# Row sums laid along the output by TensorE instead of by way of DRAM, in a fused attention and two-MoE kernel

## The chip, the cores and the metric

The kernel runs on one core of a Trainium2 chip. Its time is the device time of one execution in microseconds (us), the median of several runs. The core has five instruction streams that run side by side and meet by semaphores: TensorE (PE in the profile, its weight loads PEld), VectorE (DVE), ScalarE (ACT), GpSimd (POOL), and SyncE (SP), which here only issues DMAs. Each stream is issued in its own order.

## The reference

Three layers follow each other. Attention keeps, in each row of scores, those that are not below the 32nd largest, and takes the softmax over them:

```python
scores = scale * np.matmul(q, k.transpose(0, 1, 3, 2))        # 4 batches, 8 heads, 576 x 576, head_dim 64
kth = np.partition(scores, -32, axis=-1)[..., -32:-31]
scores = np.where(scores >= kth, scores, -1000000000.0)
attn = np.exp(scores - np.max(scores, axis=-1, keepdims=True))
attn = attn / (np.sum(attn, axis=-1, keepdims=True) + 1e-09)
x = np.matmul(attn, v)                                        # becomes 2304 tokens x 512
x = (x @ w_a) * (x @ w_b) @ w_out                             # first MoE layer, d_ff 1536
# second layer: each token goes to the best of 8 experts by a normalised dot product:
out[mask] = gate_w[mask, None] * (np.maximum(x[mask] @ w1[e], 0.0) @ w2[e])
```

The change lies in the division by the row sum and in what stands around it.

## The kernel before, in words

Work is laid out in three stretches of one program: attention with the first MoE layer in its gaps, the rest of the first MoE layer with routing, and the experts.

Attention goes by pairs of heads and by *parts* of a batch. A part (`prep`, line 268) is one pair of heads and 256 query columns ("A", "B"), with 64 more where it has a tail ("T"); the order of parts stands in `SEQ` (line 28), four pairs for each entry, 32 parts in all, 16 of them with a tail. A part without a tail has 4 *row blocks* of 128 queries, one with a tail has 5; there are 144 row blocks. One *step* of the main loop (line 820) takes one row block through each of its stages, each stage at another distance:

- `scores` (348), two steps ahead: two halves of 288 columns, matmuls into PSUM and an eviction by ScalarE (364). The halves use the pool `sc` of one bank, all other PSUM tiles of attention (turns of K and Q, turns of weights, mix) share the pool `tr` of `NTR = 3` banks. Two further pools of two banks belong to the MoE layer.
- `topk` (367), at the step itself and the next: four MAX8 and three MATCH_REPLACE8 over 576 columns on DVE, then the threshold (389). Row n's first half and row n-1's second half are issued alternately (lines 849 to 852).
- `softmax` (391), two steps later: Relu on ScalarE (396) makes a penalty, POOL negates the maximum (397) and subtracts the penalty (398), ScalarE takes the exponential and sums it into `o.sm` (400).
- `turn` (402), three steps later up to step 18, then four (`TL0`, `TL`, `S1`): five transposes by PE in two tiles (417), evicted into `o.wt` (420).
- `mix` (438), in the step after the last turn of the part: 10 matmuls with V, evicted to `o.xsb` (449). The first four parts (`F0 * NP`) run it at once.
- `sums` (423), three steps after the last row of a part, at the head of DVE's work of that step: add 1e-9 (428), reciprocal (429). The result lies with queries on partitions, the output of `mix` has queries along columns. So the reciprocals are stored to DRAM, transposed (430), and read back by one or two DMAs that repeat them over 64 partitions each (433, 436) into `o.xR`.
- `finish` (455), `LATE = 2` steps after `mix`: POOL multiplies `xsb` by `xR` (457), splits the product into two float32r parts, and SyncE stores them (466, 467) for the first MoE layer. Four pairs of a batch's part finished make a group of tokens ready.

Within a step the order is written out by hand (lines 841 to 925, under `manual_schedule`): loads of V (841), `sums` and `topk` (845 to 852), K and Q work, then five slots (892): first tile of turns, first half of scores, second tile of turns, mix, second half of scores. `soft` is the generator of `softmax`: its first part (Relu, negation, subtraction) is issued after slot 0, the exponential after slot 2. After every piece, `background` (752) issues matmuls of the first MoE layer from a budget per step (`STEP`). SyncE issues in the order of the program too, except where a priority moves a DMA ahead.

Other names that the trace shows: raw weights of the first MoE layer arrive by L496 and are converted by DVE (516, 518), ScalarE (519) and POOL (523, 533) until 330 us; the split weights go to `wab_d` in DRAM and come back as `wab` for each group of 256 tokens (589); `xg` (577) are a group's tokens; L650 are the matmuls with `wab`; `route` (673) stores rows at L707.

Of the kernel before, what the change touches and what calls it, by code (L numbers as in the profile page):

```python
# [10 lines left out]
F32 = mybir.dt.float32  # L11
# [17 lines left out]
LAG = 2  # L29
AHEAD_L = 8  # L30
TL = 4
LATE = 2
STEP = 4.8
TL0 = 3
S1 = 19
F0 = 1
# [46 lines left out]
def fused_kernel(  # L83
# [37 lines left out]
    xl_d = drm.tile([P, NP, NT], F32, name="xl_d")  # L121
    wab_d = drm.tile([2, NF, P, 2 * KC * P], F32, name="wab_d")
    kT_d = drm.tile([B * NP, P, 2 * S], F32, name="kT_d")
    rc_d = drm.tile([3 * B * NP, 5, P], F32, name="rc_d")
    row_d = drm.tile([NT + 1, RW], F32, name="row_d")
    ids_d = drm.tile([NE * STRIDE, 2], I32, name="ids_d")

# [69 lines left out]
    with ExitStack() as ph:  # L197
        wk = ph.enter_context(tc.tile_pool(name="wk", bufs=2, side="right"))
        ps = ph.enter_context(tc.tile_pool(name="ps", bufs=2, space=PSUM, side="right"))
        NTR = 3  # L200

        fill = wk.tile([P, S], F32, name="z", bufs=ZB).bitcast(I32)[:, : NE * STRIDE * 2 // P]
        dve.memset(fill, NT)
# [144 lines left out]
        def scores(t):  # L348
            o = t.o
            t.s = wk.tile([P, S], F32, name="s", bufs=SB)  # L350
            for j in range(2):
                if j and t.n == 0:
                    p = ps.tile([P, 512], F32, name="tr", bufs=NTR)[:, :288]
                else:
                    p = ps.tile([P, 288], F32, name="sc", bufs=1)
                cs = slice(j * 288, (j + 1) * 288)
                if t.kind == 2:
                    terms = [(o.qm[:, a, h, :], o.kT[:, h, cs]) for h in range(2) for a in range(2)]
                else:
                    off = (2 * t.kind + t.c) * P  # L360
                    terms = [(o.qT[:, a, off : off + P], o.kT[:, t.kind, cs]) for a in range(2)]
                for i, (l, r) in enumerate(terms):
                    pe.matmul(p, l, r, start=(i == 0), stop=(i == len(terms) - 1))  # L363
                act.activation(t.s[:, cs], p, AF.Copy, scale=SCALE)  # L364
                yield 0.12 * len(terms)
# [55 lines left out]
                yield 0.107 * n5  # L421

        def sums(o):

            o.xR = wk.tile([P, 320], F32, name="xR", bufs=2)
            d = rc_d[o.n]
            sl = slice(0 if o.M else 4, 5 if o.tail else 4)
            dve.tensor_scalar(o.rc[:, sl], o.sm[:, sl], 1e-9, None, op0=OP.add)
            dve.reciprocal(o.rc[:, sl], o.rc[:, sl])
            sp.dma_start(d[sl].rearrange("c p -> p c"), o.rc[:, sl])  # L430
            if o.M:
                src = d[0:4].rearrange("(h c) p -> h (c p)", h=2)
                sp.dma_start(o.xR[:, :256], src.unsqueeze(1).to_broadcast([2, 64, 256]))
            if o.tail:
                src = d[4].rearrange("(h j) -> h j", h=2)
                sp.dma_start(o.xR[:, o.M : o.N], src.unsqueeze(1).to_broadcast([2, 64, 64]))

        def mix(o):
            N = o.N
            o.xsb = wk.tile([P, 320], F32, name="xsb")  # L440
            o.xh = wk.tile([P, 320], F32R, name="xh", bufs=1)
            p = ps.tile([P, 512], F32, name="tr", bufs=NTR)
            for c in range(5):
                ks = slice(0, P) if c < 4 else slice(64, P)
                for h in range(2):
                    pe.matmul(  # L446
                        p[h * 64 : h * 64 + 64, :N], o.vs[ks, h, c], o.wt[h][ks, c, :N], start=(c == 0), stop=(c == 4)
                    )
            act.activation(o.xsb[:, :N], p[:, :N], AF.Copy)
            later(now[0] + LATE, finish, o)  # L450
            yield N / 100

# [352 lines left out]
        def later(step, fn, *args):  # L805
            due.append((step, fn, args))
# [10 lines left out]
        cur = none  # L817
        thresholds = [none]
        coming = []
        for step in range(-AHEAD_L, NRW + TL + 5):  # L820
            now[0] = step
            if step + AHEAD_L < NRW:
# [7 lines left out]
            if 0 <= step + AHEAD_P < NRW:  # L830
# [7 lines left out]
                o.left += 1  # L838
                live[step + AHEAD_P] = Rows(o, kind, c, slot)
                live[step + AHEAD_P].n = step + AHEAD_P  # L840
            for ahead, todo_v in ((1, load_v),):
                if 0 <= step + ahead < NRW and rows[step + ahead][3]:
                    with tc.high_priority(offset=FG):
                        todo_v(made[rows[step + ahead][:3]])
            with tc.high_priority(offset=FG):
                if 0 <= step - 3 < NRW and rows[step - 3][4]:
                    sums(live[step - 3].o)
                if 0 <= step < NRW:
                    cur = topk(live[step], FOLD[step % len(FOLD)])
                for _ in range(4):  # L850
                    next(thresholds[0], None)
                    next(cur, None)
                if step == NRW:
                    thresholds[0] = none
                elif 0 <= step < NRW:
                    thresholds[0] = cur
# [13 lines left out]
                    coming.pop(0)  # L870
            while 0 <= step + AHEAD_Q < NRW and live[step + AHEAD_Q].o in flips:
                flip_next()
            soft = softmax(live[step - 2]) if 0 <= step - 2 < NRW else none
            i = step - (TL0 if step < S1 else TL)
            if i != turned[0] + 1:
                i = -1
# [15 lines left out]
            for slot_, g in enumerate((tg, sg, tg, mg, sg)):  # L892
# [1 line left out]
                    mixes.pop(0)  # L894
                    mg = none
                with tc.high_priority(offset=FG):
                    if slot_ in (0, 2):
                        next(soft, None)
                    if slot_ < 3:
                        conv.stage()  # L900
# [348 lines left out]
```

## Time and profile before

| | us |
|---|---|
| median of 3 runs | 1520.99 (1520.69 to 1521.65) |
| the profiled execution's own time | 1534.14 |
| its span, first to last instruction | 1532.3 |
| PE busy | 1211.9 (79%) |
| DVE busy | 927.3 (61%) |
| ACT busy | 790.1 (52%) |
| POOL busy | 755.2 (49%) |

The page also shows the span in 40 slices of 38.3 us; each digit is the busy share of a slice in tenths, for PEclk the granted clock, for DMA the mean share of the 16 DMA engines:

```profile
PE   4566666658688787878778797877999997999997
DVE  6979668758688777978686888911100013554451
ACT  4655555556565666666555575633433233444441
POOL 5655567765454655655565556544444432112210
PEclk9856777779899989999899899978999999999999
DMA  6432356566468856575587875927987823645440
```

DVE's high digits end in slice 26, near 1000 us: there the last row block is over. Attention takes the first 1045 us with its last stores; PE's nines after that are the rest of the first MoE layer and the experts. An engine's busy share is an average over such stages, and idle time of an engine that nobody waits for costs nothing.

### The profile page before, as it was taken

What the parts mean: (1) busy time and instruction counts of PE and PEld (TensorE: products, weight loads), DVE (VectorE), ACT (ScalarE), POOL (GpSimd) and SP (SyncE); (2) the same over time, 40 slices, a digit from 0 to 9 for tenths busy, and PEclk for the clock granted to TensorE, in tenths of its full rate; (3) what the DMA queues carried; (4) which work ended last, traced back from release to release, by engine and by line L of the source; (5) the groups of instructions that cost most, each with busy time, mean ns of one, the idle gap of its engine ahead of it and who ended that gap; (6) DMA issues with size and microseconds to landing.
All of it is one profiled execution on the core that took longest, in us unless ns stands there. A gap on an engine that the chain in (4) does not pass through costs nothing. (4 is left out here: it accounts for less than half of the span.)

```text
span 1532.3 us, 22337 instructions
## 1 busy us (share of the span) xinstructions
PE 1211.9 (79%) x7400; PEld 1010.9 (66%) x7401; DVE 927.3 (61%) x2022; ACT 790.1 (52%) x1885; POOL 755.2 (49%) x1164
## 2 busy tenths in 40 slices
PE   4566666658688787878778797877999997999997
PEld 3444554546566666767656576756888886888886
DVE  6979668758688777978686888911100013554451
ACT  4655555556565666666555575633433233444441
POOL 5655567765454655655565556544444432112210
PEclk9856777779899989999899899978999999999999
DMA  6432356566468856575587875927987823645440
GB/s 200 122 86 60 123 141 155 176 185 146 128 182 131 131 148 167 156 211 131 123 152 148 181 144 149 181 68 259 318 288 232 244 73 112 204 165 177 158 139 17
DMA packets 150889, 241.75 MB, mean 158 GB/s; under 512 B 43853, under 2 KB 96205, under 8 KB 150770
## 3 DMA queue, kind: packets, MB, share of 16 engines
q1 hardware_dynamic: 146610, 230.00, 56.2%
q0 software_dynamic: 4160, 10.29, 2.1%
q8 instruction: 59, 0.97, 0.4%
q14 instruction: 60, 0.49, 0.2%
HBM read 200.10 MB, written 40.93 MB: 157 GB/s over the span
## 5 line engine op out<-in xcount | busy, mean ns | idle before, releaser
L650 PE MATMUL ab<-xg,wab 128*128 128x256 f32 x2592 | 406.9, 303 | 77.0 <-DMA wab<-wab_d 45.1
L650 PEld LDWEIGHTS ab<-xg,wab 128*128 128x128 f32 x2592 | 362.2, 204 | 93.6 <-DMA wab<-wab_d 28.5
L398 POOL TENSOR_TENSOR z<-s,z 128x576 f32<-128x576 f32 x144 | 205.7, 1428 | 260.3 <-ACT z L396 252.9
L384 DVE MAX8 t<-y 128x8 f32<-128x576 f32 x432 | 311.3, 748 | 3.1
L363 PE MATMUL sc<-kT,qT 128*128 128x288 f32 x510 | 148.6, 374 | 107.8 <-ACT s L364 100.9
L387 DVE MATCH_REPLACE8 y<-t,y 128x576 f32<-128x576 f32 x288 | 213.9, 743 | 0.0
L363 PEld LDWEIGHTS sc<-kT,qT 128*128 128x128 f32 x510 | 94.7, 223 | 151.4 <-ACT s L364 132.3
L417 PE MATMUL tr<-ident,z 128*128 128x128 f32 x720 | 150.1, 313 | 54.9 <-ACT z L400 29.9
L400 ACT ACTIVATE z<-z,bi 128x576 f32<-128x576 f32 x144 | 111.2, 772 | 123.9 <-POOL z L398 122.9
L420 ACT ACTIVATE wt<-tr 128x384 f32<-128x384 f32 (+2 forms) x320 | 127.8, 413 | 42.1 <-PE tr L417 39.3
L417 PEld LDWEIGHTS tr<-ident,z 128*128 128x128 f32 x720 | 99.7, 159 | 69.9 <-ACT z L400 33.0
L621 PE MATMUL x<-wo,gh 128*128 128x512 f32 x432 | 141.4, 410 | 0.0
L364 ACT ACTIVATE s<-sc 128x288 f32<-128x288 f32 x287 | 116.1, 405 | 25.8 <-PE sc L363 24.3
L1032 PE MATMUL y<-u,hT 128*128 128x512 f32 (+1 forms) x528 | 128.0, 396 | 0.4 <-DVE hT L1137 0.4
L384 DVE MAX8 t<-s 128x8 f32<-128x576 f32 x144 | 107.1, 744 | 30.9 <-ACT s L364 30.9
L955 DVE TENSOR_TENSOR u<-raw,u 128x1024 fp32r<-128x1024 f32 x64 | 76.3, 1221 | 79.1 <-ACT u L954 79.0
L1004 POOL DMA_INDIRECT out_dram<-o,ids x24 | 24.1, 1005 | 199.0 <-ACT o L1003 197.1
L659 POOL TENSOR_TENSOR gab<-gab 128x256 f32<-128x256 f32 x108 | 81.7, 756 | 80.3 <-ACT gab L654 64.3
L446 PE MATMUL tr<-wt,vs 128*64 128x256 f32 (+3 forms) x640 | 113.9, 502 | 1.8 <-ACT kT L321 1.1
L396 ACT ACTIVATE z<-s,bi 128x576 f32<-128x576 f32 x144 | 112.3, 780 | 0.3 <-DVE bi L389 0.3
L1032 PEld LDWEIGHTS y<-u,hT 128*128 128x128 f32 (+1 forms) x528 | 89.8, 174 | 27.5 <-DVE hT L1137 0.5
L387 DVE MATCH_REPLACE8 y<-t,s 128x576 f32<-128x576 f32 x144 | 106.9, 743 | 0.0
(169 smaller groups left out, 1912.5 us busy)
## 6 DMA issues: line engine op xcount, KB each, us to landing
wab<-wab_d SPq DMA_DIRECT2D x192, 512.0 KB
raw<-in_moe_w_dram SPq DMA_DIRECT2D x28, 1024.0 KB
wab_d<-wab SPq DMA_DIRECT2D x24, 512.0 KB
kT_d<-kT SPq DMA_DIRECT2D x16, 576.0 KB
kT<-kT_d SPq DMA_DIRECT2D x16, 576.0 KB
vs<-in_v_dram SPq DMA_DIRECT2D x32, 256.0 KB
raw<-in_moe_w_a_dram SPq DMA_DIRECT2D x12, 512.0 KB
raw<-in_moe_w_b_dram SPq DMA_DIRECT2D x12, 512.0 KB
```

What stands on the lines that cost most here:

```text
L363: pe.matmul(p, l, r, start=(i == 0), stop=(i == len(terms) - 1))
L364: act.activation(t.s[:, cs], p, AF.Copy, scale=SCALE)
L384: dve.max(v, cur)
L387: dve.match_replace(out=rest, in_to_replace=v, in_values=cur, imm_value=LOWEST)
L396: act.activation(t.w, t.s, AF.Relu, bias=t.bi[:, 1:2], scale=-HUGE)
L398: pool.tensor_tensor(t.w, t.s, t.w, op=OP.subtract)
L417: pe.transpose(pt[:, i * P : (i + 1) * P], t.w[:, k0 : k0 + P], ident)
L420: act.activation(th[:, sl, w], pv[:, :, src], AF.Copy)
L446: pe.matmul(p[h * 64 : h * 64 + 64, :N], o.vs[ks, h, c], o.wt[h][ks, c, :N], start=(c == 0), stop=(c == 4))
L621: pe.matmul(px[t], g[:, ts], wo[:, w, f], start=(f == 0 and i == 0), stop=(f == NF - 1 and i == 2))
L650: pe.matmul(p[:, i], wt[:, a, c, :], xg[x][:, c, :], start=(j == 0), stop=(j == len(terms) - 1))
L1032: pe.matmul(p[:m], (hi, lo)[a], u[:, b, f % 4, :], start=(f == 0 and i == 0), stop=(f == NF2 - 1 and i == 2))
```

## The change

Reciprocals no longer go through DRAM: `rc_d` and its 32 stores and 48 reads are gone. A new function `along`, called in `mix` after the eviction, makes matmuls whose stationary operand is a column of reciprocals repeated 64 times and whose moving operand is the identity, so that each of 64 output partitions gets the reciprocals along its columns; ScalarE copies the result into `o.xR`. `sums` keeps its two DVE instructions and is called five steps after a part's last row, three for the first four parts. The exponential of a row is issued at the head of the next step, before `sums` and `topk`, and the first part of `softmax` after slot 1. V's load is issued two steps after a part's first row, and one step ahead of it as before only for the first two parts. `finish` follows in the step of `mix` (`LATE = 0`). Scores take their tiles from `tr`, which has four banks now; `sc` is gone.

```diff
@@ -29,7 +29,7 @@
 LAG = 2
 AHEAD_L = 8
 TL = 4
-LATE = 2
+LATE = 0
 STEP = 4.8
 TL0 = 3
 S1 = 19
@@ -121,7 +121,6 @@
     xl_d = drm.tile([P, NP, NT], F32, name="xl_d")
     wab_d = drm.tile([2, NF, P, 2 * KC * P], F32, name="wab_d")
     kT_d = drm.tile([B * NP, P, 2 * S], F32, name="kT_d")
-    rc_d = drm.tile([3 * B * NP, 5, P], F32, name="rc_d")
     row_d = drm.tile([NT + 1, RW], F32, name="row_d")
     ids_d = drm.tile([NE * STRIDE, 2], I32, name="ids_d")
 
@@ -197,7 +196,7 @@
     with ExitStack() as ph:
         wk = ph.enter_context(tc.tile_pool(name="wk", bufs=2, side="right"))
         ps = ph.enter_context(tc.tile_pool(name="ps", bufs=2, space=PSUM, side="right"))
-        NTR = 3
+        NTR = 4
 
         fill = wk.tile([P, S], F32, name="z", bufs=ZB).bitcast(I32)[:, : NE * STRIDE * 2 // P]
         dve.memset(fill, NT)
@@ -349,10 +348,7 @@
             o = t.o
             t.s = wk.tile([P, S], F32, name="s", bufs=SB)
             for j in range(2):
-                if j and t.n == 0:
-                    p = ps.tile([P, 512], F32, name="tr", bufs=NTR)[:, :288]
-                else:
-                    p = ps.tile([P, 288], F32, name="sc", bufs=1)
+                p = ps.tile([P, 512], F32, name="tr", bufs=NTR)[:, :288]
                 cs = slice(j * 288, (j + 1) * 288)
                 if t.kind == 2:
                     terms = [(o.qm[:, a, h, :], o.kT[:, h, cs]) for h in range(2) for a in range(2)]
@@ -421,19 +417,27 @@
                 yield 0.107 * n5
 
         def sums(o):
-
-            o.xR = wk.tile([P, 320], F32, name="xR", bufs=2)
-            d = rc_d[o.n]
             sl = slice(0 if o.M else 4, 5 if o.tail else 4)
             dve.tensor_scalar(o.rc[:, sl], o.sm[:, sl], 1e-9, None, op0=OP.add)
             dve.reciprocal(o.rc[:, sl], o.rc[:, sl])
-            sp.dma_start(d[sl].rearrange("c p -> p c"), o.rc[:, sl])
-            if o.M:
-                src = d[0:4].rearrange("(h c) p -> h (c p)", h=2)
-                sp.dma_start(o.xR[:, :256], src.unsqueeze(1).to_broadcast([2, 64, 256]))
-            if o.tail:
-                src = d[4].rearrange("(h j) -> h j", h=2)
-                sp.dma_start(o.xR[:, o.M : o.N], src.unsqueeze(1).to_broadcast([2, 64, 64]))
+
+        def along(o):
+
+
+            p = ps.tile([P, 512], F32, name="tr", bufs=NTR)
+            for s in range(0 if o.M else 2, 3 if o.tail else 2):
+                for h in range(2):
+                    w, src, js = (s * P, 2 * h + s, slice(0, P)) if s < 2 else (o.M, 4, slice(h * 64, h * 64 + 64))
+                    n = js.stop - js.start
+                    pe.matmul(
+                        p[h * 64 : h * 64 + 64, w : w + n],
+                        o.rc[js, src : src + 1].to_broadcast([n, 64]),
+                        ident[js, js],
+                        start=True,
+                        stop=True,
+                    )
+            o.xR = wk.tile([P, 320], F32, name="xR", bufs=2)
+            act.activation(o.xR[:, : o.N], p[:, : o.N], AF.Copy)
 
         def mix(o):
             N = o.N
@@ -447,6 +451,7 @@
                         p[h * 64 : h * 64 + 64, :N], o.vs[ks, h, c], o.wt[h][ks, c, :N], start=(c == 0), stop=(c == 4)
                     )
             act.activation(o.xsb[:, :N], p[:, :N], AF.Copy)
+            along(o)
             later(now[0] + LATE, finish, o)
             yield N / 100
 
@@ -817,6 +822,7 @@
         cur = none
         thresholds = [none]
         coming = []
+        soft = none
         for step in range(-AHEAD_L, NRW + TL + 5):
             now[0] = step
             if step + AHEAD_L < NRW:
@@ -838,13 +844,18 @@
                 o.left += 1
                 live[step + AHEAD_P] = Rows(o, kind, c, slot)
                 live[step + AHEAD_P].n = step + AHEAD_P
-            for ahead, todo_v in ((1, load_v),):
-                if 0 <= step + ahead < NRW and rows[step + ahead][3]:
+            for ahead in (1, -2):
+                j = step + ahead
+                if 0 <= j < NRW and rows[j][3] and (made[rows[j][:3]].n < 2) == (ahead == 1):
                     with tc.high_priority(offset=FG):
-                        todo_v(made[rows[step + ahead][:3]])
+                        load_v(made[rows[j][:3]])
             with tc.high_priority(offset=FG):
-                if 0 <= step - 3 < NRW and rows[step - 3][4]:
-                    sums(live[step - 3].o)
+                next(soft, None)
+                soft = softmax(live[step - 2]) if 0 <= step - 2 < NRW else none
+                for back in (3, 5):
+                    j = step - back
+                    if 0 <= j < NRW and rows[j][4] and (made[rows[j][:3]].n < F0 * NP) == (back == 3):
+                        sums(made[rows[j][:3]])
                 if 0 <= step < NRW:
                     cur = topk(live[step], FOLD[step % len(FOLD)])
                 for _ in range(4):
@@ -870,7 +881,6 @@
                     coming.pop(0)
             while 0 <= step + AHEAD_Q < NRW and live[step + AHEAD_Q].o in flips:
                 flip_next()
-            soft = softmax(live[step - 2]) if 0 <= step - 2 < NRW else none
             i = step - (TL0 if step < S1 else TL)
             if i != turned[0] + 1:
                 i = -1
@@ -894,7 +904,7 @@
                     mixes.pop(0)
                     mg = none
                 with tc.high_priority(offset=FG):
-                    if slot_ in (0, 2):
+                    if slot_ == 1:
                         next(soft, None)
                     if slot_ < 3:
                         conv.stage()
```

## Rows read from the trace of the kernel before

**Rows 1.** Windows view: window, us, busy PE, PEld, DVE, ACT, POOL (instructions); clock, DMA share, GB/s.
```profile
150.00:400.00 250.00, 156.26 (x873) 128.56 (x875) 179.38 (x373) 137.64 (x320) 162.19 (x189) 0.75 0.56 153
400.00:1000.00 600.00, 490.09 (x3248) 400.15 (x3246) 488.80 (x1123) 375.56 (x979) 346.03 (x573) 0.92 0.68 153
```

**Rows 2.** SyncE's waits, 0 to 1045: who for whom, us in total, times, longest.
```profile
SPq L433 <- DMA rc_d<-rc: 250.5, 26, 11.4
SPq L430 <- DVE rc L429: 64.4, 24, 7.6
...
SPq L259 <- PE tr L446: 51.9, 12, 10.9
```

**Rows 3.** Timeline of SyncE, 202 to 217: start, us, issue.
```profile
204.68 0.38 SPq L430 DMA_DIRECT2D rc_d<-rc  x1
...
206.44 0.37 SPq L496 DMA_DIRECT2D raw<-in_moe_w_out_dram  x1
...
214.82 0.51 SPq L433 DMA_DIRECT2D xR<-rc_d  x1
```

**Rows 4.** Timeline of DVE, 203 to 222; in brackets the idle time before and its end.
```profile
219.35 0.43 DVE L516 TENSOR_SCALAR w64t<-raw 128x512 int32<-128x512 int32 x1 [9.77 <-DMA raw<-in_moe_w_out_dram]
```

**Rows 5.** Waits of all engines, 400 to 1000 (columns as in rows 2).
```profile
DVE rc L428 <- ACT z L400: 84.5, 17, 13.9
...
ACT z L400 <- POOL z L398: 72.4, 61, 6.5
```

**Rows 6.** The page's costliest groups: count, busy us, mean ns, idle before, releaser.
```profile
L396 ACT ACTIVATE z<-s,bi 128x576 f32<-128x576 f32 x144 | 112.3, 780 | 0.3 <-DVE bi L389 0.3
```

**Rows 7.** PE's waits, 400 to 1000.
```profile
PE sc L363 <- ACT s L364: 59.8, 69, 4.5
PE ab L650 <- DMA wab<-wab_d: 25.8, 8, 7.7
```

**Rows 8.** DVE's waits, 150 to 400.
```profile
DVE w64t L516 <- DMA raw<-in_moe_w_out_dram: 27.7, 3, 9.8
...
DVE w64t L516 <- DMA raw<-in_moe_w_a_dram: 14.0, 5, 9.4
```

**Rows 9.** PE's waits, 150 to 400.
```profile
PE ab L650 <- DMA wab<-wab_d: 10.8, 1, 10.8
```

**Rows 10.** Timeline of SyncE, 988 to 1045.
```profile
999.26 0.52 SPq L433 DMA_DIRECT2D xR<-rc_d  x1
...
1000.40 0.37 SPq L707 DMA_DIRECT2D row_d<-xr  x1
```

**Rows 11.** Waits of all engines, 1000 to 1045.
```profile
POOL xr L706 <- DMA row_d<-xr: 11.4, 1, 11.4
...
POOL xsb L457 <- DMA xR<-rc_d: 10.4, 1, 10.4
```

**Rows 12.** Groups by shape, 0 to 1045, and L449's copies (min/median/max ns).
```profile
L417 PE MATMUL tr<-ident,z 128*128 128x128 f32 x720 | 150.1, 313 | 54.9 <-ACT z L400 29.9 <-ACT wt L420 20.9 <-ACT xsb L449 2.5
...
L446 PEld LDWEIGHTS tr<-wt,vs 128*64 128x64 f32 x512 | 42.7, 173 | 39.8 <-issue 20.3 <-PE sc L363 2.3 <-ACT kT L321 1.9
...
L449 ACT ACTIVATE xsb<-tr x32: 361/401/439, 61.7 to 1030.3; 128x256 f32<-128x256 f32 x16, 128x320 f32<-128x320 f32 x16
```

**Rows 13.** Waits of all engines, 0 to 150.
```profile
PE tr L417 <- ACT z L400: 26.7, 12, 3.6
...
DVE rc L428 <- ACT z L400: 11.2, 4, 4.3
```

**Rows 14.** Windows view of the hundred us in which DVE is busiest after 150.
```profile
900.00:1000.00 100.00, 84.49 (x565) 68.74 (x566) 91.22 (x215) 65.28 (x164) 56.47 (x105) 0.93 0.77 162
```

**Rows 15.** Timelines of DVE (ends of row blocks) and PE (a mix), 608 to 626.
```profile
614.89 0.13 DVE L389 TENSOR_SCALAR bi<-t 128x1 f32<-128x1 f32 x1
...
619.98 0.13 DVE L389 TENSOR_SCALAR bi<-t 128x1 f32<-128x1 f32 x1
...
623.33 2.53 PE L446 MATMUL tr<-wt,vs 128*64 128x256 f32 x20
```

## The prediction, made before the result was known

> **What bounds the kernel now.** I read the stage table first, then SyncE's own waits, then the compute engines' waits stage by stage.
>
> In attention's second stage, 150 to 400 us [rows 1], no engine is above 72% (DVE 179.38, POOL 162.19 of 250) and PE's granted clock is 0.75, between its levels of 1.2 and 2.4 GHz: everybody waits. From 400 to 1000 PE is busy 490.09 and DVE 488.80 of 600, at 0.92: two engines at 82% that hold each other up.
>
> Who holds them up stands in SyncE's waits [rows 2]: 250.5 us before L433, for the store of the row sums (L430) to land before they are read back, 26 waits of 9.6 us; 64.4 before L430 itself, for DVE's reciprocal; 51.9 before V's load (L259), for the mix that still reads the old buffer. SyncE issues in order, so for a third of the 1045 us every other load is queued behind these three. In one case [rows 3] the store goes out at 204.68, the read-back at 214.82, and a load of raw weights, issued at 206.44 right behind the store, lets DVE go on only at 219.35 [rows 4], 12.9 us later, after 9.77 us of idle time. So the store delays also what is already issued.
>
> DVE's own biggest wait is another one: 84.5 us in 17 times from 400 to 1000 before the sums' addition (L428), for the part's last exponential [rows 5]. It looks like the prize, and I do not count it as one: the sums stand at the head of DVE's step, and ScalarE's Relu, which consumes what DVE makes, waited for DVE 0.3 us in all 144 rows [rows 6]. DVE is early; it stalls there because ScalarE and PE are late, and if only the sums moved it would stall a little later.
>
> What makes those two late from 400 to 1000: 72.4 us of ScalarE before the exponential [rows 5], for POOL's subtraction issued half a step earlier; 59.8 us of PE before scores, for the eviction of the single `sc` bank, and 25.8 for the first MoE's weights [rows 7].
>
> **The change part by part.** The sum is made against the profiled run's own time, 1534.14 us (span 1532.3); the median of 1520.99 is 0.9914 of it, and I scale at the end.
>
> 1. *The DRAM exchange goes* (32 stores, 48 reads), and V's load moves, for all but the first two parts, behind the mix that frees its buffer; so the waits at L433, L430 and most of L259 leave SyncE. V's two DMAs go three steps back in its order, past K's, Q's and the weights' loads; the mix wants them six or seven steps later, some 30 us, so this costs nothing. What is late next is the load itself; a loss I exclude, since the same bytes move in fewer DMAs.
> 150 to 400: DVE's waits for raw weights are 27.7 + 14.0 = 41.7 us [rows 8], PE's for weights 10.8 [rows 9]. Bounds: 52.5 if all go; 10.8 if only PE's counts, because POOL's conversions would take the time anyway. I take 35, nearer the upper: DVE, PE and ScalarE stand together, but a load that no exchange delays still takes time.
> 400 to 1000: 25.8 us of PE [rows 7]; bounds 0 and 25.8; I take 22.
> 1000 to 1045: the row store at L707 goes out at 1000.40, directly behind the read-back of 999.26 [rows 10], and POOL waits 11.4 us for it; then the last read-back keeps POOL 10.4 us [rows 11]. No row work is left to cover these. Bounds 10 and 21.8; I take 18.
>
>    Against this stands a rule. The Trainium skill, DMA: Bandwidth & Descriptors, section "Latency and other measured facts", puts the fixed cost of a DMA at about 2 us, most of it the receipt from memory, so a store of 2 KB would hold SyncE about 2 us. By it the exchange would explain a fifth of the 75 us above, and the time would come out near 1500. The trace disagrees: 250.5 us in 26 waits [rows 2]. I go by the trace.
>
> 2. *Exponential half a step later, Relu in slot 1, four shared banks.* POOL's subtraction has the other evictions of the step to hide behind, so ScalarE's 72.4 us before the exponential should mostly go; and a score tile waits for the eviction four tiles back and not for the one just before it. Both lie in one loop, so they don't add. Bounds: 0 (the loop is paced elsewhere) and 59.8, PE's wait; DVE's 111 us of idle time here would allow that. I take 20, since PE is the nearest to full and gets new work (next). If the subtraction's cover is gone, the old 72.4 come back. A loss, turns waiting for a bank that scores now hold, I bound by giving this gain back.
>
> 3. *New work.* `along` issues 4 fp32 matmuls for a part without tail and 6 with, two instructions each, as mix's 320 matmuls make 640: 16 x 8 + 16 x 12 = 320. Nearest rows [rows 12]: weight loads of 64 columns, 42.7/512 = 0.08 us each, and fp32 turns of 128 columns, 150.1/720 = 0.21; so 27 to 67 us of PE. I take 0.12, near the weight load, since two heads' column halves can overlap: 38 us. PE idles 110 us from 400 to 1000, so I put 10 on the path; bounds 0 and 67. The 32 copies of 0.40 us [rows 12] on ScalarE (13 us) fit into its idle 224 us. DVE's two instructions are the same, two steps later; `sm` and `rc` have three buffers and come round three parts (over 12 rows) later, so nobody waits for them. `finish` two steps earlier makes POOL wait for the two copies; behind it stands only the next row's negation and subtraction, which wait for Relu in the next step anyway: nothing. Group 0 is ready two steps earlier, in the stretch that waits for weights: nothing, at best -5.
>
> 4. *The first parts.* There the sums stay three steps back while the exponential moves later, and turns follow three steps after their row, directly behind it. From 0 to 150 DVE waits 11.2 us in 4 times at L428 and PE 26.7 us for the exponential [rows 13]. Bounds: -11 (DVE's wait goes) and +38 (both double). I take +5, as DVE paces this stage.
>
> Sum: -35 - 22 - 18 - 20 + 10 + 5 = -80; 1534.1 - 80 = 1454; times 0.9914: **1442 us**.
>
> **The rivals.**
> A, *the loop keeps its pace.* POOL covers the raw weights; banks and exponential free time that ScalarE and PE don't turn into speed. For it: DVE's big wait is slack already. Against it: in one place [rows 4] DVE stands 9.77 us with nothing to do. Gained are only PE's weights (10.8 + 25.8) and the tail (18); `along` costs its whole 38, the first parts 10: -54.6 + 48 = -7, 1527, scaled 1514.
> B, *DVE becomes the pacer.* With all loads early and ScalarE unblocked, 150 to 1000 could run as its best hundred does, DVE 91.22 of 100 [rows 14]: (179.38 + 488.80) / 0.912 = 733 for 850, -117; with tail and first parts -130: 1404, scaled 1392. For it: the two best engines are only 82% busy. Against: that hundred had no raw conversion.
> C, *slower: PE waits for the sums.* The mix, which waited only for turns and V, is now followed in PE's order by matmuls that need DVE's reciprocal of the same step; scores, turns and all MoE matmuls stand behind. If DVE were one row block late (5.09 us, 614.89 to 619.98 [rows 15]), 28 parts would cost 142 us: 1534 - 80 + 142 = 1596, scaled 1582. It decides from 80/28 = 2.9 us a part. Against it: DVE reached the block of the mix at 619.98, and PE began that mix at 623.33, 3.35 us later [rows 15]; and Relu, two slots before, needs DVE to be as far. For it: this margin is about the deciding size, and PE may run ahead of ScalarE by four banks.
> The Trainium skill, TensorE: Matmul & The Clock Gate, "Part 3: Packing small matmuls", says matmuls start and end strictly in program order; by it nothing could slip past the waiting one.
> That the exchange stays in part can't be: no DMA of it is left.
>
> **How the numbers follow.** Chances: forecast 0.52, A 0.20, B 0.20, C 0.06, rest 0.02. The forecast's own range is 1410 to 1478. The range reaches to B at 1390 and on the upper side to 1500, where A begins; the bounds of term 1 (21 to 100 in all) and term 3 (0 to 67) span about as much. A measurement of this kernel tells 0.2% (3 us) from no change. Faster takes the forecast, B, 0.15 of A and the rest: 0.89; A's remainder gives same 0.03 and, with C, slower 0.08.
>
> **What would show it.** Right: no wait on SyncE above 5 us but for buffers; DVE's waits for raw weights under 15 us; DVE's row blocks over near 920 instead of 1000; ScalarE's wait before the exponential under 20 us from 400 to that end; DVE's wait at the sums gone, and part of it back as waits for scores. Wrong: idle time before `along`, ended by DVE; PE's waits for `tr` evictions in place of those for `sc`; weights still late with SyncE free, which would mean that the DMA engines and not the queue were the limit; or a first stage longer by more than 15 us.

## The result and the profile after

The changed kernel takes **1388.25 us** (1386.05 to 1390.8; before, in the same runs, 1521.32): 0.912 of before, 95% interval 0.9095 to 0.9145. So it is 133 us faster where 79 were forecast, 1.75 us below the range's end. Its profiled execution took 1389.12 us.

The page's slices first (DVE and PEclk, as in the table before), then the windows view:

```profile
DVE  6979999988998999998878989511000125444440
...
PEclk9856878889989999998989989999999989999999
```

```profile
150.00:400.00 250.00, 198.77 (x1297) 169.37 (x1298) 235.26 (x494) 176.51 (x424) 198.54 (x244) 0.85 0.60 191
400.00:850.00 450.00, 391.32 (x2833) 334.75 (x2831) 400.80 (x916) 320.27 (x828) 292.44 (x487) 0.93 0.52 166
```

In the second stage DVE went from 72% busy [rows 1] to 94%, and PE, busy 198.77 us instead of 156.26, was granted a clock of 0.85 instead of 0.75 (as a mean, between its two levels). In the third DVE went from 81% to 89%. The higher clock is no main cause: the 2592 matmuls with `wab`, a third of PE's busy time, took 406.9 us before and 407.3 after. Mix (113.9 to 94.7) and scores (179.0 to 164.6) got shorter; why is open. DVE's last row block ends 115 us earlier, at 886.9 instead of 1002.1 (the timeline of DVE):

```profile
886.88 0.15 DVE L385 TENSOR_SCALAR bi<-t 128x1 f32<-128x1 f32 x1
```

By the ends of row blocks 16 and 40, counted from 0 (127.2 and 340.5 before, 124.1 and 293.7 after), the first stage gained 3 us, the second 44, the rest of attention 68. What follows DVE's last block shrank from 530.2 us to 500.5. Together that is 145 us and not 133, since the profiled execution before was 13 us above its median.

SyncE's waits, 0 to 1045, have none for `rc_d` any more, but V's load (L258) waits 118.8 us where it waited 51.9 [rows 2]:

```profile
SPq L594 <- PE ab L655: 183.4, 91, 8.6
SPq L258 <- PE tr L450: 118.8, 29, 10.6
```

Both lines are waits for a buffer to come free (the first was 53.4 us before).

The compute engines' waits in the same stretch:

```profile
DVE t L380 <- ACT s L360: 45.2, 30, 5.7
...
ACT z L396 <- POOL z L394: 40.1, 48, 2.0
...
PE tr L302 <- POOL qs L217: 34.4, 10, 6.0
...
POOL xsb L462 <- ACT xR L440: 26.9, 16, 3.4
...
DVE rc L421 <- ACT z L396: 18.6, 5, 8.0
```

The first and the last line are DVE's waits for scores and at the sums; over the same stretch they were 30.9 and 132.0 us before, so 163 us became 64. The third and fourth are new: PE waits before the turns of Q (L302) for POOL's splits of Q, and POOL waits in `finish` for the copied reciprocals. New work by shape (`along`'s matmuls and loads, 27 us and 17 us):

```profile
L432 PE MATMUL tr<-ident,rc 128*64 128x128 f32 x256 | 21.5, 290 | 2.9 <-ACT wab L536 2.4 <-ACT wt L416 0.6
...
L432 PEld LDWEIGHTS tr<-ident,rc 128*64 128x64 f32 x256 | 13.6, 138 | 17.1 <-issue 5.3 <-ACT wt L416 4.3 <-ACT wab L536 2.9
...
L432 PE MATMUL tr<-ident,rc 64*64 64x64 f32 x64 | 5.4, 248 | 0.0
L432 PEld LDWEIGHTS tr<-ident,rc 64*64 64x64 f32 x64 | 3.2, 135 | 2.9 <-issue 2.9
```

### The profile page after: what moved, and what is told of

Its sections match the earlier page's. It is cut to its first block, busy times and chain, and to the rows that moved or that the text cites. A ratio compares the mean times of both kernels' runs of the same rounds, so it can differ in the third digit from the quotient of the medians.

```text
span 1387.4 us, 22987 instructions
## 1 busy us (share of the span) xinstructions
PE 1180.6 (85%) x7720; PEld 1016.2 (73%) x7721; DVE 933.4 (67%) x2022; ACT 807.0 (58%) x1917; POOL 758.0 (55%) x1164
## 2 busy tenths in 40 slices
DMA packets 125706, 236.98 MB, mean 171 GB/s; under 512 B 22765, under 2 KB 71021, under 8 KB 125586
## 5 line engine op out<-in xcount | busy, mean ns | idle before, releaser
L655 PE MATMUL ab<-xg,wab 128*128 128x256 f32 x2592 | 407.3, 303 | 32.7 <-ACT wab L536 11.7
L655 PEld LDWEIGHTS ab<-xg,wab 128*128 128x128 f32 x2592 | 363.7, 205 | 43.0 <-ACT wab L536 13.4
L413 PE MATMUL tr<-ident,z 128*128 128x128 f32 x720 | 147.0, 308 | 56.9 <-ACT z L396 43.6
L359 PE MATMUL tr<-kT,qT 128*128 128x288 f32 x512 | 138.1, 356 | 7.2 <-ACT qT L336 4.1
L360 ACT ACTIVATE s<-tr 128x288 f32<-128x288 f32 x288 | 118.3, 411 | 25.1 <-PE tr L359 22.8
L965 DVE TENSOR_TENSOR u<-raw,u 128x1024 fp32r<-128x1024 f32 x64 | 76.3, 1221 | 63.8 <-ACT u L964 63.8
L626 PE MATMUL x<-wo,gl 128*128 128x512 f32 x216 | 94.9, 439 | 19.9 <-POOL gl L613 19.9
L359 PEld LDWEIGHTS tr<-kT,qT 128*128 128x128 f32 x512 | 96.7, 225 | 16.9 <-ACT qT L336 5.9
L613 POOL TENSOR_TENSOR gl<-gab,gh 128x256 fp32r<-128x256 f32 x108 | 83.0, 769 | 45.7 <-ACT gh L613 35.2
```

What stands on the lines that cost most here:

```text
L413: pe.transpose(pt[:, i * P : (i + 1) * P], t.w[:, k0 : k0 + P], ident)
L626: pe.matmul(px[t], g[:, ts], wo[:, w, f], start=(f == 0 and i == 0), stop=(f == NF - 1 and i == 2))
L655: pe.matmul(p[:, i], wt[:, a, c, :], xg[x][:, c, :], start=(j == 0), stop=(j == len(terms) - 1))
```

## The experiments

Each was timed in three rounds against the kernel before; ratios have 95% intervals, a ratio of 0.01 is 15.2 us.

### Parts alone on the kernel before

`e1_along_only`: reciprocals by `along` instead of the DRAM exchange, nothing else.

```diff
-            sp.dma_start(d[sl].rearrange("c p -> p c"), o.rc[:, sl])
...
             act.activation(o.xsb[:, :N], p[:, :N], AF.Copy)
+            along(o)
```

> The kernel before, with nothing changed but the exchange: along in mix in place of the DRAM store and read-back; sums stay 3 steps back, exponential, V's load, banks and LATE as before. Theory Q (queue: the exchange alone held everybody up through SyncE): nearly the whole gain, 1395 to 1415 us. Theory P (DVE becomes the pacer only when the exchange, the exponential's wait and the sums' stall are all gone; the parts help each other): about 1440 to 1465, the raw-weight waits of DVE between 150 and 400 gone, DVE's waits at the sums still above 80 us. Theory S (DVE's stall at the sums was no slack): at or above 1470.

`e2_banks_only`: scores in `tr` with four banks.

```diff
-        NTR = 3
+        NTR = 4
...
-                    p = ps.tile([P, 288], F32, name="sc", bufs=1)
+                p = ps.tile([P, 512], F32, name="tr", bufs=NTR)[:, :288]
```

> The kernel before with four shared banks for scores and turns, and nothing else. Theory P: PE's wait for the sc eviction (about 124 us over attention) falls below 40, the time by little, 1500 to 1518, since SyncE and the sums still hold the others. If the banks carry the unforeseen gain (theory B): below 1490. Theory Q: 1515 to 1525.

`e3_exp_only`: exponential at the next step's head, Relu after slot 1.

```diff
+                next(soft, None)
+                soft = softmax(live[step - 2]) if 0 <= step - 2 < NRW else none
...
-                    if slot_ in (0, 2):
+                    if slot_ == 1:
```

> The kernel before with only the Relu in slot 1 and the exponential at the head of the next step; sums stay 3 steps back, directly behind it, exchange and banks as before. Theory P: ScalarE's wait before the exponential falls below 40 us, but DVE's wait at the sums grows from 132 us, no gain or a loss, 1515 to 1545. If the exponential alone frees the loop (theory E): below 1500.

Measured: 1448.82 (0.9539, 0.9505 to 0.9574), 1490.1 (0.9813, 0.9774 to 0.9852) and 1478.44 (0.9713, 0.9669 to 0.9757): 70, 28 and 44 us by the ratios. All three keep most of DVE's stall at the sums (99.0, 102.3 and 96.7 us, for 132.0 before). In the third, ScalarE's wait before the exponential fell; all waits, 0 to 1045:

```profile
DVE rc L428 <- ACT z L400: 96.7, 24, 18.1
...
ACT z L400 <- POOL z L398: 38.9, 45, 12.7
```

The three sum to 142, near the 134 of the whole. That is an accident, as the next runs show.

### Parts taken out of the changed kernel

`e4_exchange_back`: the exchange again, `finish` four steps after `mix` to leave time for it. `e14_exchange_own_bank`: the same with scores in their own bank. `e5_own_bank`: only scores in their own bank.

```diff
+            sp.dma_start(d[sl].rearrange("c p -> p c"), o.rc[:, sl])
...
-            along(o)
-            later(now[0] + LATE, finish, o)
+            later(now[0] + (2 if o.n < F0 * NP else 4), finish, o)
```

> The changed kernel with the exchange through DRAM put back in place of along (sums 5 steps back, finish 4 steps after mix, 2 for the first four parts, so that the exchange has the same four steps as before); all else as changed. Theory Q: at least 1490. Theory P: 1440 to 1475, SyncE's wait before the read-back back at some 250 us. Theory S (late sums make the gain): 1390 to 1420.

> The changed kernel with the exchange through DRAM back (1438 us so far) and, now, scores in a bank of their own as well. Theory Cushion (four shared banks let PE run ahead across the stalls that the exchange makes, and so are worth something only beside it): 1455 to 1475. Theory Loop (their worth alone came from the old place of the exponential, which made ScalarE late with evictions): 1434 to 1444.

> The changed kernel with scores in a bank of their own again and three for the rest; all else as changed. Alone, on the kernel before, the four banks were worth 29 us. Theory Add (each part removes its own place in a chain of waits, so prices add): 1410 to 1425 us, PE's waits for score evictions back above 60 us. Theory One-loop (the step as I put it: banks and exponential lie in one loop and don't add): 1388 to 1400.

Measured: 1438.09 (0.9459, 0.9409 to 0.9508), 1443.66 (0.9477, 0.942 to 0.9534), 1385.83 (0.9098, 0.905 to 0.9145). Against the changed kernel the exchange costs 52 us, with SyncE's and DVE's old waits back (SyncE's, 0 to 1045; all, 150 to 400):

```profile
SPq L430 <- DMA rc_d<-rc: 298.4, 32, 13.2
```

```profile
DVE w64t L513 <- DMA raw<-in_moe_w_b_dram: 30.9, 4, 11.1
```

The 52 are too few: `finish` is not in `mix`'s step here, and that step turns out below to cost 24; against the kernel that avoids it the exchange costs 75.

The banks are worth nothing in the change and 3 us beside the exchange, less than the runs can tell, although PE then waits 44.5 us for the single bank's eviction. That wait was read as a cost [rows 7]; here it is none.

`e6_exp_early`: Relu and exponential in their old slots. `e7_sums_early`: sums three steps back for all parts. `e8_v_early`: V's load as before.

```diff
-                    if slot_ == 1:
+                    if slot_ in (0, 2):
```

```diff
-                    if 0 <= j < NRW and rows[j][4] and (made[rows[j][:3]].n < F0 * NP) == (back == 3):
+                    if 0 <= j < NRW and rows[j][4] and (back == 3):
```

> The changed kernel with Relu after slot 0 and the exponential after slot 2 of the same step as before; all else as changed, sums 5 steps back. Alone the move was worth 41 us. Theory Add: 1420 to 1435 us, ScalarE's wait for the subtraction back near 100 us. Theory One-loop: 1388 to 1405.

> The changed kernel with the sums 3 steps back for all parts, directly behind the exponential; all else as changed. Theory Slack (DVE's stall at the sums is time it has to spare, as the prediction put it): 1386 to 1396 us, although DVE's wait at the sums is back above 80 us. Theory Pacer (in the changed kernel DVE sets the pace, so its stall counts now): above 1415.

> The changed kernel with V's load one step ahead of the part's first row for all parts, as before. The prediction costs this at some of SyncE's time: SyncE would stand before the load until the mix two parts back has read the buffer, with the weights' loads behind it. Theory Queue: 1395 to 1410 us with PE's waits for weights back above 15 us. Theory Nothing (SyncE waits for that mix at either place): 1385 to 1392.

Measured: 1451.11 (0.9525, 0.9478 to 0.9572), 1421.88 (0.9345, 0.9301 to 0.9389), 1386.97 (0.9105, 0.9061 to 0.915). The old places of Relu and exponential cost 62 us in the change, for 44 alone. V's place is worth nothing: its wait for the old buffer was 117.7 us with the early load. The sums' place is worth 34, and the stall stands in the trace (0 to 1045):

```profile
DVE rc L421 <- ACT z L396: 109.9, 27, 10.5
```

### Is DVE's stall at the sums slack?

`e16_along_late_sums`: the kernel of `e1_along_only` and, beside that, only the later sums.

```diff
-                if 0 <= step - 3 < NRW and rows[step - 3][4]:
-                    sums(live[step - 3].o)
+                for back in (3, 5):
...
```

> The kernel before with along in place of the exchange and the sums 5 steps back (3 for the first four parts); exponential, banks, V's load and LATE as before. Theory Pair (late sums are worth nothing while the exponential lies in its old place, and some 34 us once it is moved): 1444 to 1454, as with along alone (1449), DVE's wait at the sums gone and turned into waits for scores. Theory Separate (late sums are worth their 34 us anywhere): 1410 to 1420.

Measured: 1418.51 (0.9315, 0.9257 to 0.9373), 34 us by the ratios below `e1_along_only`. So the later sums pay without the moved exponential, and the theory that the two work only as a pair falls. The waits (0 to 1000) of `e1_along_only`, then of this kernel:

```profile
DVE rc L424 <- ACT z L399: 99.0, 28, 10.0
...
DVE t L383 <- ACT s L363: 7.3, 5, 2.2
```

```profile
DVE t L383 <- ACT s L363: 48.1, 33, 6.0
DVE rc L424 <- ACT z L399: 23.9, 5, 11.6
```

106.3 us of waits became 72.0, 34 less, as much as the gain. Of the 75 us that left the sums, 41 came back as waits for scores, as the forecast's "it would stall a little later" has it; the other 34 did not.

How near DVE is to being the pace was measured by giving it more: one more MAX8 in each row block (0.75 us, 107 us in all), in the kernel before (`e12_before_dve_more`) and in the changed one (`e13_after_dve_more`).

```diff
+                if r == 0:
+                    dve.max(wk.tile([P, 8], F32, name="j8", bufs=1), cur)
```

> The kernel before with one MAX8 over 576 columns more per row block (0.75 us, 144 times, 107 us of DVE work, result unused). Theory Slack (before the change DVE is not the pacer; it has to spare what it stands at the sums): 20 to 60 us slower, 1540 to 1580, DVE's wait at the sums shrinks from 132 us to below 70. If DVE was the pacer all along: 90 to 107 us slower.

> The changed kernel with the same extra MAX8 per row block. Theory Pacer (the change made DVE the pacer): 85 to 107 us slower, 1473 to 1495. If PE and ScalarE still pace: 20 to 60 us slower, as in the kernel before.

Measured: 1545.73 (1.0148, 1.0114 to 1.0182) and 1422.37 (0.9341, 0.9312 to 0.937): 23 and 34 us, about a fifth and a third of what was added. The second was expected far higher if DVE were the pacer. Before, a fifth of such work came out as time: neither all nor nothing. The windows view of before, then of the changed kernel with the added work:

```profile
400.00:850.00 450.00, 366.35 (x2422) 298.31 (x2418) 361.97 (x827) 279.86 (x735) 261.93 (x425) 0.92 0.66 153
```

```profile
400.00:850.00 450.00, 384.39 (x2715) 329.66 (x2714) 444.12 (x985) 309.83 (x807) 283.50 (x464) 0.91 0.51 160
```

DVE can be filled to 444.12 of 450; the changed kernel left 49 us of this stretch unused. Even in the kernel that fills DVE so far, Relu waited for DVE only 4.3 us in the whole span (the waits of `e13_after_dve_more`), 1.4 of them from 400 to 850:

```profile
ACT z L394 <- DVE bi L387: 4.3, 4, 1.9
```

So this wait can't tell whether DVE has time to spare.

### What of the exchange costs

`e9_store`: the changed kernel and, beside `along`, the old store of the reciprocals, which nobody reads. `e10_store_read`: also a small DMA that reads a part of it back, for which SyncE waits until the store has landed; nobody uses it.

```diff
+            sp.dma_start(d[sl].rearrange("c p -> p c"), o.rc[:, sl])
+            junk = wk.tile([P, 64], F32, name="junk", bufs=2)
+            sp.dma_start(junk, d[0:2, 0:64].unsqueeze(1).to_broadcast([2, 64, 64]))
```

> The changed kernel with the store of the reciprocals to DRAM (4-byte pieces) added back after the sums, and nobody waiting for it. Theory Queue (the exchange costs because SyncE waits for the store): 1386 to 1396. Theory Packets (the store holds the DMA engines, and what is issued behind it comes late): 1405 to 1440, waits for weights behind it back.

> As the run with the store, and SyncE reads 64 columns of it back into an unused tile, so that it waits for the store as in the kernel before; nobody waits for the tile. Theory Queue: 1415 to 1445 us, SyncE's wait for the store back at some 300 us. Theory Packets: within 8 us of the run with the store alone.

Measured: 1434.61 (0.9433, 0.9399 to 0.9468) and 1455.33 (0.9561, 0.9535 to 0.9588): the store alone costs 48 us, SyncE's wait for its landing (261.8 us in all) and the small read 19 more. The timeline of SyncE, then of DVE, in the kernel with the store alone:

```profile
179.26 0.38 SPq L425 DMA_DIRECT2D rc_d<-rc  x1
179.74 0.47 SPq L504 DMA_DIRECT2D raw<-in_moe_w_a_dram  x1
...
223.47 0.38 SPq L425 DMA_DIRECT2D rc_d<-rc  x1
...
224.51 0.38 SPq L504 DMA_DIRECT2D raw<-in_moe_w_b_dram  x1
```

```profile
193.14 0.43 DVE L524 TENSOR_SCALAR w64t<-raw 128x512 int32<-128x512 int32 x1 [8.97 <-DMA raw<-in_moe_w_a_dram]
...
238.55 0.43 DVE L524 TENSOR_SCALAR w64t<-raw 128x512 int32<-128x512 int32 x1 [10.19 <-DMA raw<-in_moe_w_b_dram]
```

Loads issued 0.5 and 1.0 us behind a store reach DVE 13.4 and 14.0 us later. The answer on DMA for the changed kernel has for the same loads, from issue to landing (last number, median):

```profile
raw<-in_moe_w_a_dram SPq DMA_DIRECT2D x9, 512.0 KB, 4.5
raw<-in_moe_w_b_dram SPq DMA_DIRECT2D x9, 512.0 KB, 4.9
```

Over the whole span, waits for transfers that came late grew from 4.4 us to 23.9 at DVE for raw weights, from 4.5 to 16.3 at PE for `wab` and from 4.8 to 11.4 at POOL for the stored rows: 38 us, near the 45 between the two profiled executions. The delay behind the store need not be all of their cause: the store also makes SyncE wait for DVE's reciprocal, 63.8 us in 20 times, which no run takes apart from it.

### Smaller questions

`e17_relu_slot0`: the changed kernel with Relu after slot 0. `e18_along_twice`: all matmuls of `along` made twice.

```diff
-                    if slot_ == 1:
+                    if slot_ == 0:
```

```diff
-            for s in range(0 if o.M else 2, 3 if o.tail else 2):
+            for s in list(range(0 if o.M else 2, 3 if o.tail else 2)) * 2:
```

> The changed kernel with Relu, negation and subtraction after slot 0 as before, the exponential still at the head of the next step. Theory Distance (what counts is that evictions stand between subtraction and exponential): 1384 to 1396, ScalarE's wait for the subtraction no larger than 41 us. Theory Slot (Relu behind the first score half is what helps, since scores leave PE's way earlier): 1400 to 1430.

> The changed kernel with every matmul of along issued twice into the same place: 320 more instructions, 27 us of PE busy by the trace of the changed kernel. Theory of the prediction's step 3 (a quarter of along's PE time is on the path): 1390 to 1400. If PE is the pacer: 1410 to 1420. If along is hidden: 1386 to 1390.

Measured: 1405.82 (0.9231, 0.9175 to 0.9286), 17 us of loss, so Relu's slot matters beside the exponential's: of the 62 us of both, 45 are left for the exponential. Its trace loses 30 us by the end of row block 40 (324.2 for 293.7) and gains 14 back (why was not followed up); and 1399.78 (0.9189, 0.9134 to 0.9244), 10 us for another 23 us of PE.

### Finish in mix's own step

One sum did not close: `e16_along_late_sums` took 1418, and `e6_exp_early`, which has banks, V's load and `finish` in `mix`'s step on top, 1451. `e20_exp_early_late2` is `e6_exp_early` with `LATE = 2`; `e19_finish_later` is the changed kernel with `finish` one step after `mix`.

```diff
-            later(now[0] + LATE, finish, o)
+            later(now[0] + (LATE if o.n < F0 * NP else 1), finish, o)
```

> The changed kernel with Relu and exponential in their old slots (slot 0 and 2) and finish two steps after mix as before; so along, late sums, V's load and banks of the change. With finish in mix's step the same kernel took 1451; along and late sums alone on the kernel before, with finish two steps later, took 1418. Theory 'finish': what costs the 32 us between these is finish in mix's step, whose wait on POOL lies ahead of the subtraction that a late exponential has no time to wait for: 1413 to 1428. Rival 'banks': the four shared banks (or V's load) cost it when Relu and exponential stand in slots 0 and 2: 1443 to 1453.

> The changed kernel with finish one step after mix (the first four parts still at once). Theory 'POOL waits': issued in mix's own step, finish holds POOL until mix, along and ScalarE's copy of the reciprocals are done (about 33 us in all, with Q's splits behind it that turns wait for, 27.4 us of PE), and that is on the path: 1370 to 1382, POOL's wait for the copies under 8 us. Rival 'hidden': POOL has that much to spare in the changed kernel: 1385 to 1391, with the same waits gone.

Measured: 1405.72 (0.9282, 0.9243 to 0.932) and **1357.78** (0.8963, 0.8918 to 0.9008). The second beats the changed kernel by 24 us (by the ratios) and the kernel before by 158. In both cases `finish` in `mix`'s step was the cost (37 us there, 24 here), and a larger one than expected. The place of it in the changed kernel, timeline of all engines:

```profile
410.47 3.06 PE L450 MATMUL tr<-wt,vs 128*64 128x320 f32 x20
...
413.46 0.92 PE L432 MATMUL tr<-ident,rc 128*64 128x128 f32 x12
...
414.94 0.88 POOL L462 TENSOR_TENSOR xsb<-xsb,xR 128x320 f32<-128x320 f32 x1 [2.38 <-ACT xR L440]
...
416.46 0.87 POOL L217 TENSOR_TENSOR xR<-xsb,xh 128x320 fp32r<-128x320 f32 x1
...
417.83 0.86 POOL L217 TENSOR_TENSOR qs<-qr,qs 128x320 fp32r<-128x320 f32 x1
...
418.74 1.30 PE L302 MATMUL tr<-identr,qs 128*128 128x128 f32 x6 [2.30 <-POOL qs L217]
419.25 1.41 POOL L394 TENSOR_TENSOR z<-s,z 128x576 f32<-128x576 f32 x1
```

POOL waits 2.38 us for mix, `along` and the copy; behind it in POOL's order stand the split of Q, for which PE then waits 2.30, and the next row's subtraction. With `finish` a step later both waits shrink (all waits, 0 to 1045, now `e19_finish_later`; the changed kernel's stand in the section on the result):

```profile
DVE t L380 <- ACT s L360: 17.6, 13, 3.2
...
PE tr L302 <- POOL qs L217: 7.2, 7, 3.7
```

```profile
400.00:850.00 450.00, 408.00 (x3036) 346.54 (x3034) 431.16 (x997) 335.63 (x883) 310.96 (x521) 0.97 0.57 178
```

DVE is now 96% busy here, so of this stage little is left to win around DVE. What the new places of exponential and Relu are worth with `finish` out of the way is the difference of `e20_exp_early_late2` and this kernel, 48 us (`finish` two steps after `mix` in one, one in the other). All waits of `e20_exp_early_late2`, 0 to 1045:

```profile
ACT z L396 <- POOL z L394: 117.7, 96, 6.5
DVE t L380 <- ACT s L360: 44.2, 30, 5.8
...
PE tr L359 <- ACT s L360: 27.0, 27, 2.8
```

In `e19_finish_later` the three are 42.6, 17.6 and 2.6. ScalarE stands 75 us less before the exponential; the evictions of scores stand behind it in ScalarE's order, and DVE waits 27 us less for them, PE 24.

## Why the prediction was right or wrong

The runs make a ladder whose rungs add up to the result (us of 1521, by the ratios; a rung is uncertain by some 5 to 11, so the third is not told from nothing):

| step | forecast | measured | from |
|---|---|---|---|
| exchange gone, `along` in its place | -64 | -70 | `e1_along_only` |
| sums later | 0 | -34 | to `e16_along_late_sums` |
| four banks, V's load | part of -20 | -5 | to `e20_exp_early_late2` |
| exponential and Relu | part of -20 | -49 | to `e19_finish_later` |
| `finish` in mix's step | 0 | +24 | to the changed kernel |
| first parts | +5 | -3 | row block 16; inside the rungs above |

**The step that failed** is the reading of DVE's 84.5 us [rows 5]: "It looks like the prize, and I do not count it as one". From Relu's 0.3 us of waiting for DVE [rows 6] it was concluded that DVE is early and its stall slack. But Relu comes two steps after the row block, and even with DVE busy 444.12 of 450 us it waited for DVE only 4.3 us in all (`e13_after_dve_more`), so its wait says nothing of DVE's slack. At 82% busy DVE can't make up every stall: taking 75 us from the sums' stall gave 34 as time, and adding 107 us to DVE cost a fifth of them. Worth is a share here, and the forecast put the share at zero.

**Term 2 was mis-sized**, -20 for -54. That exponential and banks don't add was right: 44 and 28 alone, 54 together. It was sized on PE's 59.8 before scores [rows 7], which costs nothing in `e5_own_bank`; the row that counted was ScalarE's 72.4 before the exponential [rows 5]: when that wait fell (117.7 to 42.6 us over attention), DVE's and PE's waits for scores fell with it. In the changed kernel it is still 25.6 us from 400 to DVE's last block, where under 20 was to be the sign of being right. Why the banks give 28 alone and so little beside later sums (5 in the table, 3 between `e4_exchange_back` and `e14_exchange_own_bank`) was not settled.

**`finish` for nothing was wrong** in the other direction. The forecast named POOL's wait for the two copies and, behind it, only the negation and the subtraction; it overlooked Q's splits in POOL's queue, for which PE turns wait. That wait and its like are 24 us.

**Term 1 was right** in sum, -64 with `along` and -70 measured, and in the main in mechanism. Of 67 us that the exchange's store and SyncE's wait for it cost in the changed kernel, 48 come with the store alone, which delays what is issued behind it, as the forecast read from one place [rows 3, 4], and makes SyncE wait for DVE; how these two share the 48 is open. The waits that the term counted went: DVE's for raw weights from 41.7 us to 4.1 between 150 and 400, PE's for `wab` (10.8 and 25.8) to none up to DVE's last block. The Trainium skill, DMA: Bandwidth & Descriptors, "Latency and other measured facts", has about 2 us fixed for a DMA; the runs disagree, since SyncE waited 9.3 us on average for such a store to land (298.4 us in 32 waits in `e4_exchange_back`). By the profiled executions, 88 us apart, the tail gained 24 us in `e1_along_only` (506.6 after DVE's last block, for 530.2) and 18 were forecast, but the second stage gained 20 there and not 35, and 400 to the end of DVE's rows made up for it. V's part was wrong in the trace (the wait grew to 118.8) and right in the time (nothing). `along` cost 27 us of PE for the forecast's 38, and a repeat 10 of time, as forecast.

**The rivals.** A is refuted by the exponential's 49. C is refuted: in the changed kernel the idle time before `along`'s matmuls was ended by ScalarE or by issue, never by DVE (the rows of L432 above). B came out nearest, in time (1392) and in its arithmetic: from 150 us to its last row block DVE was busy 672.6 of 736.9 us, 91%, where B had 91.22 of 100 and 733 us. What B says of the pace does not hold strictly: with 107 us more DVE work the changed kernel lost 34, so DVE still had idle time to fill. The end on 1388 is several errors: two gains too small by 34 each, 6 in term 1 and 5 for the first parts, less a loss of 24 left out; that they end so near the range's edge is luck, since without that loss the time is 1358.

## What to carry to other kernels

Don't write off an engine's stall as slack because its consumer doesn't wait: where two engines are 80% busy and hold each other up, give the suspect engine a little more work and see what share comes out as time. That share is a first guess of what its stall is worth and not more: here a fifth of added work came out, and 34 of the 75 us that were taken away. When an operation is moved, list everything that is issued behind it on its engine, not only its own chain; here `finish` one step later is worth 24 us with no work saved. Gains of parts measured alone need not add: banks gave 28 alone and nothing that the runs can tell in the end.

## What the runs showed of the hardware

A store of 2 to 2.5 KB from a tile with one value of 4 bytes for each partition and column, 512 or 640 pieces, kept SyncE waiting 9.3 us on average for its landing (298.4 us in 32 waits, `e4_exchange_back`), and in the two places shown of `e9_store`, 512 KB loads issued within 1 us behind it arrive after 13.4 and 14.0 us, where their median is 4.5 to 4.9 without such stores. Thirty-two of them cost 48 us even when nobody reads them, with SyncE's waits for what they store (63.8 us in all) in the price. The page's packets under 512 B, 43853 before, 22765 in the changed kernel and 41709 with the store alone, show these pieces in a count that bytes (241.75, 236.98 and 237.07 MB) hide. The Trainium skill, DMA: Bandwidth & Descriptors, "Why small descriptors are slow (HBM only)", gives a fixed overhead for each packet as a reason; the runs agree in direction, and the size is from them. A store of the same bytes in few large pieces was not tried, so that the pieces are the cause is not shown.
